# A new start-up order for a fused sliding-window attention and leaky-ReLU MLP: weights from the first microsecond, values last, sums ahead of values

## The chip, the cores and the metric

The kernel runs on one core of a Trainium2 chip. The metric is the device time of one execution in microseconds; lower is better. Five engines work side by side, each through its own list of instructions in the order in which the program gives them: TensorE (PE, matrix products, with its weight loads shown as PEld), VectorE (DVE), ScalarE (ACT), GpSimd (POOL) and SyncE (SP), which here only issues transfers. POOL and ACT issue some transfers too. All transfers run on the core's 16 DMA engines. Waits between engines are by semaphore.

## The reference

A sliding-window attention over 8 batches of 8 heads, 576 tokens and a head size of 64, and behind it an MLP on the 4608 tokens with 512 features, 2048 hidden units and a leaky ReLU:

```python
scores = scale * np.matmul(q, k.transpose(0, 1, 3, 2))
mask = np.abs(pos[:, None] - pos[None, :]) <= 32
scores = np.where(mask, scores, -1000000000.0)
attn = np.exp(scores - np.max(scores, axis=-1, keepdims=True))
attn = attn / (np.sum(attn, axis=-1, keepdims=True) + 1e-09)
x = np.matmul(attn, v)                  # (8, 8, 576, 64)
x = x.transpose(0, 2, 1, 3).reshape(4608, 512)
h = x @ w_in                            # 512 x 2048
out = np.maximum(0.01 * h, h) @ w_out   # 2048 x 512, float32
```

## The kernel before

**Tiling.** A unit of attention work has a number `i` from 0 to 63: batch `i // 8`, half of the sequence (288 tokens) `(i // 4) % 2`, and pair of heads `i % 4`; two heads (p and p+4) share the 128 partitions. Keys and values of a pair are laid out block-diagonally in `kbd` and `vbd` (two buffers each, for odd and even batches), nine blocks of 64 tokens. The zeros around the blocks are written once per buffer, by `clear` on ScalarE, a memset on VectorE (`kbd[0]`, L123), or memsets on POOL for the second buffers (L439, L454).

**One unit.** `cast_qk` (L167) turns loaded queries and keys into bfloat16, `transposes` (L186) turns them on TensorE, ScalarE copies the results out (L194 queries, L200 keys), and `place_keys` (L212, VectorE, two copies) puts the keys into `kbd`. `score(i)` makes five matmuls into `ps` (L227, one buffer), the exponential on ScalarE (L233, into `e`) and the product with the band mask on POOL (L237, into `pr`). `weighted(i)` makes the column sums by a matrix of ones (L261 and L264, or L259 where `join` has added the two parts beforehand, from unit 12 on), five value products into `x` (L271), the reciprocal of the sums on VectorE (L277) and the product `x * r` into `xT` (L279). `x` and `s` have one PSUM buffer each, and so each sum waits until the reciprocal before it has read `s`. `cast_v` copies values into `vbd`, on ScalarE (L175) in the start-up and on POOL (L177) later.

**The MLP.** For each half of a batch (288 tokens, group `g`) `h_tile(g, f)` makes four matmuls over the 512 features for each of 16 blocks `f` of hidden units (L290), and ScalarE's leaky ReLU writes `gT` (L294). `o_tile(j)` makes 16 matmuls of 512 columns for 128 tokens (L307), copies the sum out on ScalarE (L312) and stores it. The first `h_tile` of a half needs `xT` of all four pairs of that half.

**Order.** The schedule is written out by hand. The start-up runs from L88 to L424: loads on SP; constants; then casts, transposes and scores of batch 0 among each other; chunks of the weights (`load_w_in`, four chunks of 512 hidden units, two transfers each; `load_w_out`, four chunks) issued by POOL between its other work. These transfers convert from float32 to bfloat16. `keep_busy(n)` issues matmuls whose results nobody reads. Then come `h_tile(0, ·)` with units 4 to 7 between the tiles, and `h_tile(1, ·)` with the transposes of batch 1. Loads of batch 1 wait for weights by a transfer of four bytes that reads the weight tile (`behind` in `load_qk` and `load_v`).

After that a list `plan` holds the rest of the MLP's tiles with their costs, and `due` the times, in the plan's own clock of matmul time, at which `step()` does the next attention unit; `spend` compares the two before every four matmuls (0.864 of the plan's clock for output tiles). `step()` makes, in this order, the `join` of the next unit, transposes, `score(i + 2)`, `weighted(i)`, and the casts and loads that `PLAN` names.

Of the kernel before, what the change touches and what calls it, by code (L numbers as in the profile page):

```python
# [9 lines left out]
FP32 = mybir.dt.float32  # L10
# [6 lines left out]
def kernel(  # L17
# [12 lines left out]
    nc = tc.nc  # L30
# [18 lines left out]
    cast = ctx.enter_context(tc.tile_pool(name="cast", bufs=1))  # L49
    attn = ctx.enter_context(tc.tile_pool(name="attn", bufs=2))  # L50
    kt = ctx.enter_context(tc.tile_pool(name="kt", bufs=4))
    prob = ctx.enter_context(tc.tile_pool(name="prob", bufs=4))
    outp = ctx.enter_context(tc.tile_pool(name="outp", bufs=4))
    PS = bass.MemoryType.PSUM
    mmps = ctx.enter_context(tc.tile_pool(name="mmps", bufs=4, space=PS))
# [29 lines left out]
            )  # L85
        vf[b, p] = t

    load_qk(0, 0)  # L88
    load_qk(0, 1)
    load_v(0, 0)  # L90
    load_qk(0, 2)
    load_v(0, 1)
    load_qk(0, 3)
    load_v(0, 2)
    load_v(0, 3)


    ident_f = const.tile([128, 128], FP32)
# [18 lines left out]
    def clear(t, p):  # L117
        flat = t[:, p].rearrange("p n j -> p (n j)")
        nc.scalar.activation(
            out=flat, in_=zero.to_broadcast([128, NB * 128]), func=AF.Copy,  # L120
        )

    nc.vector.memset(kbd[0], 0.0)  # L123
    clear(vbd[0], 0)
    clear(vbd[0], 1)

# [3 lines left out]
    ]  # L132
    ODD = [32, 0]

    win = const.tile([128, 3, 128], BF16)
    nc.gpsimd.memset(win, 1.0)
    for lo in (0, 64):
        w = win[lo:lo + 64]
        nc.gpsimd.affine_select(
            out=w, in_=w, compare_op=ALU.is_ge, fill=0.0,  # L140
            base=0, channel_multiplier=-1, pattern=[[0, 3], [1, 128]],
        )
        nc.gpsimd.affine_select(
            out=w, in_=w, compare_op=ALU.is_ge, fill=0.0,
            base=2 * W, channel_multiplier=1, pattern=[[0, 3], [-1, 128]],
        )
    win_f = win.rearrange("p n c -> p (n c)")
    mask = [const.tile([128, NCOL], BF16, name=f"mask{i}") for i in range(2)]

    def make_masks():  # L150
        for hf in range(2):
            lo = W * (hf + 1)
            nc.gpsimd.tensor_copy(out=mask[hf][:, 0:HALF], in_=win_f[:, lo:lo + HALF])
            nc.gpsimd.tensor_copy(out=mask[hf][:, HALF:NCOL], in_=win_f[:, 0:NCOL - HALF])


    RING = 4 * HALF
    xT = const.tile([128, NPAIR, RING], BF16)
    w_in_bf = const.tile([128, DMC, DFF], BF16)
    w_out_bf = const.tile([128, FFC, DMODEL], BF16)  # L160


    qT = {}
# [55 lines left out]
    def where(i):  # L219
        return i // 8, (i // 4) % 2, i % 4  # L220

    def score(i):
        b, hf, p = where(i)
        ps = scps.tile([128, 1024], FP32, name="ps")
        c0 = 512 - HALF
        for blk, q0, n in WIN[hf]:
            nc.tensor.matmul(  # L227
                ps[:, c0:c0 + n], kbd[b % 2][:, p, blk],
                qT[b][:, p, q0:q0 + n], start=True, stop=True,
            )  # L230
            c0 += n
        e = attn.tile([128, NCOL], BF16, name="e")
        nc.scalar.activation(  # L233
            out=e, in_=ps[:, 512 - HALF:512 - HALF + NCOL], func=AF.Exp, scale=scale,
        )
        pr = prob.tile([128, NCOL], BF16, name="pr")
        nc.gpsimd.tensor_mul(pr, e, mask[hf])  # L237
        probs[i] = pr, None

    def join(i):  # L240


        hf = where(i)[1]
        pr = probs[i][0]
        both = prob.tile([128, HALF], BF16, name="both")
        o0 = ODD[hf]
        o1 = o0 + NCOL - HALF
        nc.vector.tensor_add(both[:, o0:o1], pr[:, o0:o1], pr[:, HALF:NCOL])  # L248
        rest = slice(0, o0) if o0 else slice(o1, HALF)
        nc.vector.tensor_copy(out=both[:, rest], in_=pr[:, rest])  # L250
        probs[i] = pr, both

    def weighted(i):
        b, hf, p = where(i)
        pr, both = probs.pop(i)
        x = xps.tile([128, HALF], FP32, name="x")
        s = xps.tile([128, HALF], FP32, name="s")
        if both is not None:
            nc.tensor.matmul(s, ones_bd, both, start=True, stop=True)  # L259
        else:  # L260
            nc.tensor.matmul(  # L261
                s, ones_bd, pr[:, 0:HALF], start=True, stop=False, skip_group_check=True,
            )
            nc.tensor.matmul(  # L264
                s[:, ODD[hf]:ODD[hf] + NCOL - HALF], ones_bd, pr[:, HALF:NCOL],
                start=False, stop=True, skip_group_check=True,
            )
        c0 = 0
        for n_, (blk, q0, n) in enumerate(WIN[hf]):
            a = q0 - HALF * hf  # L270
            nc.tensor.matmul(  # L271
                x[:, a:a + n], vbd[b % 2][:, p, blk, :], pr[:, c0:c0 + n],
                start=(n_ == 0), stop=(n_ == len(WIN[hf]) - 1), skip_group_check=True,
            )
            c0 += n
        r = attn.tile([128, HALF], FP32, name="r")
        nc.vector.reciprocal(r, s)  # L277
        t0 = (b * S + hf * HALF) % RING
        nc.vector.tensor_mul(xT[:, p, t0:t0 + HALF], x, r)  # L279

# [34 lines left out]
    def keep_busy(n):  # L315


        t = mmps.tile([128, 512], FP32, name="mm", tag="mm")
        for _ in range(n):
            nc.tensor.matmul(t, ones_bd, mask[0][:, 0:512], start=True, stop=True)  # L320


    NC = 2 * NPAIR * B
    JOINED = 12
    state = {"tp": 8, "done": 0}
    t_parts = {}


# [17 lines left out]
    def step():  # L346
# [7 lines left out]
        if b > 0:  # L354
            upto = 8 * (b + 1) + PLAN[b > 1][0][r]
            step_transposes(max(upto - 1, 8 * (b + 1)))
        if i < 7:
            score(i + 1)
        elif 8 <= i < NC - 2:
            score(i + 2)  # L360
        weighted(i)
        place_keys()
        if b > 0:
            step_transposes(upto)
# [9 lines left out]
        state["done"] += 1  # L374


    w_in_r = moe_w_in.rearrange("(a u d) f -> a d u f", a=2, d=D)
    w_out_r = moe_w_out.rearrange("(c p) f -> p c f", p=128)

    def load_w_in(f0, f1):  # L380
        for a in range(2):
            nc.gpsimd.dma_start(
                out=w_in_bf[64 * a:64 * a + 64, :, f0:f1], in_=w_in_r[a, :, :, f0:f1],
            )

    def load_w_out(i):
        c = slice(4 * i, 4 * i + 4)
        nc.gpsimd.dma_start(out=w_out_bf[:, c, :], in_=w_out_r[:, c, :])

    first = transposes(0)  # L390

    def first_pair():
        next(first)
        next(first)
        place_keys()

    cast_qk(0, 0, nc.vector)
    make_masks()
    cast_qk(0, 1, nc.vector)
    first_pair()  # L400
    first_pair()
    clear(vbd[0], 2)
    cast_v(0, 0)
    cast_qk(0, 2, nc.vector)
    score(0)
    load_w_in(0, 512)
    first_pair()
    clear(vbd[0], 3)
    cast_qk(0, 3, nc.vector)
    load_w_in(512, 1024)  # L410
    for i in range(NPAIR):
        score(i + 1)
        if i + 1 < NPAIR:
            cast_v(0, i + 1, on_act=True)
        if i < 2:
            load_w_in(1024 + 512 * i, 1536 + 512 * i)
        else:
            load_w_out(i - 2)
        if i > 0:
            keep_busy(3 if i == 1 else 2)  # L420
        weighted(i)
        if i == 0:
            first_pair()
    state["done"] = NPAIR  # L424

    for p in range(NPAIR):
        load_qk(1, p, w_in_bf[0:1, 0, 512:514] if p == 0 else None)
    keep_busy(2)  # L430
    step()
    load_w_out(2)
    load_w_out(3)
    for f in range(FFC):
        h_tile(0, f)
        if f in (2, 6, 10):
            step()
        if f % 4 == 3:
            nc.gpsimd.memset(kbd[1][:, f // 4], 0.0)  # L439
    cast_qk(1, 0, nc.vector)  # L440
    cast_qk(1, 1, nc.vector)
    for p in range(NPAIR):
        load_v(1, p, w_out_bf[0:1, 4, 0:2] if p == 0 else None)
    second = transposes(1)
    for f in range(FFC):
        h_tile(1, f)
        if f % 4 == 3:
            p = f // 4
            next(second)
            next(second)  # L450
            place_keys()
            if p + 2 < NPAIR:
                cast_qk(1, p + 2, nc.vector)
            nc.gpsimd.memset(vbd[1][:, p], 0.0)  # L454
        if f == 11:
            score(8)
    state["tp"] = 16
    score(9)
    for p in range(NPAIR):
        load_qk(2, p)  # L460

# [15 lines left out]
            at[g] = t  # L477
        t += us
    due = []
    for i in range(8, NC):  # L480
        prev = 0.9 * O_US * 4 if i < 12 else at[i // 4 - 1] - LEAD
        due.append(prev + (at[i // 4] - LEAD + (1.2 if i < 12 else 0) - prev) * (i % 4 + 1) / 4)
    clock = 0.0
    cast_v(1, 0)
    load_v(2, 0)

    def spend(us):
        nonlocal clock
        while due and due[0] <= clock:
            due.pop(0)  # L490
            i = state["done"]
            if i < 11:
                cast_v(1, i - 7)
                load_v(2, i - 7)
            step()
        clock += us

    for us, kind, g, f in plan:
# [33 lines left out]
```

## Time and profile before

| What | us |
|---|---|
| Median of 3 runs (lowest, highest) | 339.45 (339.32, 340.53) |
| The profiled execution, whole | 338.24 |
| its span, first to last instruction | 336.5 |
| TensorE busy (share) | 317.7 (94%) |
| VectorE, ScalarE, POOL busy | 232.6, 199.9, 180.3 |
| First matmul of any kind | 5.15 |
| First matmul of `h_tile(0, 0)` | 28.01 |
| First matmul of `o_tile(0)` | 48.73 |
| First matmul of `h_tile(2, 0)` | 69.58 |

The profiled execution was 1.21 us shorter than the median of the timed runs, 1.74 of it outside the span. A line of the profile's views names the engine and the kernel's line, `out<-in` by the names in the program, the shape and the count; in the views in order of time the first number is the start in microseconds from the start of the span and the second the length. What stands in square brackets is how long the engine had been idle, and what ended that. In the chain of waits every line is a piece of the chain that ended last, followed back from the end. A busy TensorE is not a TensorE at its peak, since the ends of matmuls are modelled and overlap; the distance between the starts of successive matmuls tells its pace.

### The profile page before, as it was taken

To read this page: it belongs to the slowest core of one execution; us is meant where nothing else is said; L and a number is where in the kernel's file an instruction comes from. 1 tells how busy PE (TensorE), PEld (TensorE's weight loads), DVE (VectorE), ACT (ScalarE), POOL (GpSimd) and SP (SyncE) were. 2 spreads that over 40 slices of the span, in tenths; PEclk is the share of its full clock that TensorE was granted. 3 is DMA by queue.
4 is the path that set the end of the run, shared out by engine and by line. 5 is a ranking of instruction groups with operands and counts; after the bars stand their busy time and mean duration, and the time that the engine had idled before them with its cause. 6 is when DMAs were issued, how large, how long until landed. Compare 5 with 4: busy or idle time off the path is not lost.

```text
span 336.5 us, 7011 instructions
## 1 busy us (share of the span) xinstructions
PE 317.7 (94%) x2725; PEld 215.6 (64%) x2725; DVE 232.6 (69%) x310; ACT 199.9 (59%) x432; POOL 180.3 (54%) x213
## 2 busy tenths in 40 slices
PE   2588999889999999999999999999999999999996
PEld 1346775466675767666675767667675766666653
DVE  5489653788768978797667978897677977666200
ACT  5775792275663856566564756567474656555441
POOL 7697658648755637565354646665363644221000
PEclk9999999999999999999999999999999999999999
DMA  8999989986794433553445423553311001010102
GB/s 186 215 201 222 270 195 213 268 199 178 183 180 148 139 94 99 157 163 73 126 127 156 135 68 107 165 178 73 106 29 64 33 2 62 2 62 3 62 2 94
DMA packets 60853, 42.40 MB, mean 126 GB/s; under 512 B 39700, under 2 KB 56340, under 8 KB 60820
## 3 DMA queue, kind: packets, MB, share of 16 engines
q1 hardware_dynamic: 51204, 28.32, 35.7%
q10 hardware_dynamic: 5328, 9.44, 7.8%
q0 software_dynamic: 4288, 4.20, 7.5%
q8 instruction: 21, 0.34, 0.4%
q14 instruction: 12, 0.10, 0.1%
HBM read 36.70 MB, written 9.44 MB: 137 GB/s over the span
## 4 chain that ended last, share of the span: by engine, by line
PE 83%; DMA 6%; DVE 5%; SPq 2%; ACT 2%; POOL 1%; issue 1%; ACTq 0%; DVEq 0%
PE mm L290 36%; PE mm L307 33%; PE tp L186 4%; PE x L271 4%; PE ps L227 4%; DVE r L277 3%; DMA kf<-in_k_dram 2%; DMA out_dram<-o_sb 2%; PE s L259 2%; DMA vf<-in_v_dram 2%; SPq L82 1%; SPq L71 1%; DVE xT L279 1%; ACT kT L200 0%; POOL vbd L177 0%
## 5 line engine op out<-in xcount | busy, mean ns | idle before, releaser
L277 DVE RECIPROCAL r<-s 128x288 f32<-128x288 f32 x64 | 125.2, 1957 | 55.4 <-PE s L259 47.3
L237 POOL TENSOR_TENSOR pr<-e,mask 128x544 bf16<-128x544 bf16 x64 | 77.6, 1214 | 111.9 <-ACT e L233 62.0
L290 PE MATMUL mm<-xT,w_in_bf 128*128 128x288 bf16 x1024 | 133.9, 286 | 0.0
L307 PE MATMUL mm<-w_out_bf,gT 128*128 128x512 bf16 (+2 forms) x592 | 130.1, 373 | 0.0
L290 PEld LDWEIGHTS <-w_in_bf 128*128 128x128 bf16 x1024 | 97.9, 98 | 24.8 <-issue 0.9
L294 ACT ACTIVATE gT<-mm 128x288 bf16<-128x288 f32 x256 | 99.9, 417 | 18.2 <-PE mm L290 6.7
L307 PEld LDWEIGHTS <-gT 128*128 128x128 bf16 x592 | 56.3, 98 | 59.8
L312 ACT ACTIVATE o_sb<-mm 128x512 f32<-128x512 f32 (+2 forms) x37 | 21.7, 586 | 81.3 <-PE mm L307 81.2
L233 ACT ACTIVATE e<-ps 128x544 bf16<-128x544 f32 x64 | 40.0, 625 | 27.1 <-PE ps L227 12.1
L177 POOL CAST vbd<-vf 64x576 bf16<-64x576 f32 x58 | 38.9, 670 | 2.5 <-DMA vf<-in_v_dram 0.6
L212 DVE COPY kbd<-kT 64x576 bf16<-64x576 bf16 x64 | 28.4, 444 | 11.2 <-ACT kT L200 10.6
L279 DVE TENSOR_TENSOR xT<-x,r 128x288 bf16<-128x288 f32 x64 | 29.3, 458 | 6.7
L167 POOL CAST kb<-kf 96x768 bf16<-96x768 f32 x32 | 27.5, 860 | 9.3 <-DMA kf<-in_k_dram 9.3
L248 DVE TENSOR_TENSOR both<-pr 128x256 bf16<-128x256 bf16 x52 | 27.0, 519 | 3.9 <-POOL pr L237 2.1
L227 PE MATMUL ps<-qT,kbd 128*128 128x128 bf16 (+2 forms) x320 | 26.8, 216 | 1.2 <-ACT e L233 1.2
L271 PE MATMUL x<-pr,vbd 128*128 128x128 bf16 (+2 forms) x320 | 26.3, 214 | 1.3 <-DVE xT L279 0.9
L227 PEld LDWEIGHTS <-kbd 128*128 128x128 bf16 x320 | 20.5, 101 | 8.8 <-issue 1.5
L271 PEld LDWEIGHTS <-vbd 128*128 128x128 bf16 x320 | 21.0, 100 | 5.9 <-issue 1.8
L250 DVE COPY both<-pr 128x32 bf16<-128x32 bf16 x52 | 24.6, 473 | 0.0
L194 ACT ACTIVATE qT<-tp 128x576 bf16<-128x576 bf16 x32 | 20.8, 651 | 3.3 <-PE tp L186 2.9
L200 ACT ACTIVATE kT<-tp 128x576 bf16<-128x576 bf16 x32 | 21.0, 656 | 2.9 <-PE tp L186 1.5
L186 PE MATMUL tp<-ident,qb 96*128 96x96 bf16 x192 | 14.4, 215 | 8.5 <-DVE qb L167 8.5
(37 smaller groups left out, 130.4 us busy)
## 6 DMA issues: line engine op xcount, KB each, us to landing
qf<-in_q_dram SPq DMA_DIRECT2D x32, 288.0 KB, 3.3
kf<-in_k_dram SPq DMA_DIRECT2D x32, 288.0 KB, 4.0
vf<-in_v_dram SPq DMA_DIRECT2D x64, 144.0 KB, 3.7
out_dram<-o_sb ACTq DMA_DIRECT2D x35, 256.0 KB, 2.5
w_in_bf<-in_moe_w_in_dram POOLq DMA_DIRECT2D x8, 256.0 KB, 6.5
w_out_bf<-in_moe_w_out_dram POOLq DMA_DIRECT2D x4, 512.0 KB, 11.9
out_dram<-o_sb ACTq DMA_DIRECT2D x1, 192.0 KB, 1.9
out_dram<-o_sb ACTq DMA_DIRECT2D x1, 64.0 KB, 1.6
```

What stands on the lines that cost most here:

```text
L177: nc.gpsimd.tensor_copy(out=vbd[b % 2][r, p, :, r], in_=vf[b, p][r])
L186: nc.tensor.transpose(tp[:, c], src[:, p, c].rearrange("p a d -> p (a d)"), ident[0:96, 0:96],)
L212: nc.vector.tensor_copy(out=kbd[b % 2][r, p, :, r], in_=kT[r].rearrange("p (n j) -> p n j", j=64),)
L227: nc.tensor.matmul(ps[:, c0:c0 + n], kbd[b % 2][:, p, blk], qT[b][:, p, q0:q0 + n], start=True, stop=True,)
L233: nc.scalar.activation(out=e, in_=ps[:, 512 - HALF:512 - HALF + NCOL], func=AF.Exp, scale=scale,)
L237: nc.gpsimd.tensor_mul(pr, e, mask[hf])
L271: nc.tensor.matmul(x[:, a:a + n], vbd[b % 2][:, p, blk, :], pr[:, c0:c0 + n], start=(n_ == 0), stop=(n_ == len(WIN[hf]) - 1), skip_group_c ...
L277: nc.vector.reciprocal(r, s)
L279: nc.vector.tensor_mul(xT[:, p, t0:t0 + HALF], x, r)
L290: nc.tensor.matmul(h[:, 0:HALF], w_in_bf[:, c, ts(f, 128)], xT[:, c, ds(t0, HALF)], start=(c == 0), stop=(c == DMC - 1),)
L294: nc.scalar.activation(out=gT[:, f, ds(t0, HALF)], in_=h[:, 0:HALF], func=AF.Prelu, alpha=0.01,)
L307: nc.tensor.matmul(o[:, lo:hi], gT[:, f, ds(128 * j % RING, 128)], w_out_bf[:, f, lo:hi], start=(f == 0), stop=(f == FFC - 1),)
```

## The change

Loads on SP: all queries and keys of batch 0 first, then all values. `load_w_in(0, 512)` is issued by POOL before everything else that POOL does; the other chunks and `w_out` follow between casts and mask products. `clear` runs for pairs 0 to 2 at the start. The band mask is made from one 128-column `win1` with four smaller selects, and VectorE copies it three times into `win`. For units 0 to 3 the mask product is taken in two parts straight from `win`, on VectorE for unit 3.

`weighted` is split into `sums` (sums and reciprocal) and `context` (value products and `x * r`). For units 0 to 3 `context` writes into the MLP's PSUM pool, and `r` gets four buffers, `pr` six. The start-up is written out unit by unit: sums are called before the values of the unit are cast. In the steady state `step` calls both one after the other.

```diff
+    for p in range(NPAIR):
+        load_qk(0, p)
+    for p in range(NPAIR):
+        load_v(0, p)
...
+    load_w_in(0, 512)
...
+    for p in range(NPAIR - 1):
+        clear(vbd[0], p)
     nc.vector.memset(kbd[0], 0.0)
-    clear(vbd[0], 0)
-    clear(vbd[0], 1)
...
+    nc.vector.tensor_copy(
+        out=win, in_=win1.rearrange("p (o c) -> p o c", o=1).to_broadcast([128, 3, 128]),
+    )
...
+        if i < NPAIR:
+            eng = nc.vector if i == 3 else nc.gpsimd
+            for lo, hi, at0 in PARTS[hf]:
+                eng.tensor_mul(pr[:, lo:hi], e[:, lo:hi], win_f[:, at0:at0 + hi - lo])
+        else:
+            nc.gpsimd.tensor_mul(pr, e, mask[hf])
...
+        r = recip.tile([128, HALF], FP32, name="r")
+        nc.vector.reciprocal(r, s)
+        probs[i][2] = r
+
+    def context(i):
+        b, hf, p = where(i)
+        pr, _, r = probs.pop(i)
+        if i < NPAIR:
+            x = mmps.tile([128, HALF], FP32, name="x0", tag="mm")
+        else:
+            x = xps.tile([128, HALF], FP32, name="x")
...
+        if i < NC - 2 and i not in (6, 7, 8, 9):
             score(i + 2)
-        weighted(i)
+        if probs[i][2] is None:
+            sums(i)
+        context(i)
```

The new start-up in full:

```python
cast_qk(0, 0, nc.vector)
load_w_in(512, 1024)
cast_qk(0, 1, nc.vector)
first_pair()
place_keys()
score(0)
cast_qk(0, 2, nc.vector)
first_pair()
place_keys()
score(1)
sums(0)
load_w_in(1024, 1536)
cast_qk(0, 3, nc.vector)
first_pair()
place_keys()
clear(vbd[0], 3)
score(2)
sums(1)
load_w_in(1536, 2048)
first_pair()
cast_v(0, 0, on_act=True)
place_keys()
make_masks()
score(3)
sums(2)
context(0)
cast_v(0, 1, on_act=True)
load_w_out(0)
keep_busy(4)
sums(3)
context(1)
score(4)
cast_v(0, 2, on_act=True)
load_w_out(1)
keep_busy(6)
context(2)
score(5)
cast_v(0, 3, on_act=True)
keep_busy(4)
context(3)
sums(4)
load_w_out(2)
load_w_out(3)
```

`keep_busy` now takes 288 columns a matmul, not 512, and writes `x`. Behind the start-up, queries, keys and values of batch 1 are loaded together, gated by the last chunk of `w_in`. In `h_tile(0, ·)` unit 4 to 7 come at f = 1, 5, 9 and 13: `context(i)`, then `sums(i + 1)` and `score(i + 2)`; POOL clears all of `kbd[1]` and `vbd[1]` there. `score(8)` and `score(9)` are made at f = 9 and 13 of `h_tile(1, ·)`.

Beside the first four output tiles, units 8 to 11 are divided in the `due` list: sums at 0.3, 2.4, 4.5 and 6.6 of the plan's clock (with `score(10)` and `score(11)`), then steps at 7.0, 8.7, 10.4 and 12.1, each with `cast_v(1, i - 8)` called just before it; `load_v(2, ·)` follows steps 11 to 14. Before, steps 8 to 12 fell into this stage; now unit 12 comes after it.

```diff
-    for i in range(8, NC):
-        prev = 0.9 * O_US * 4 if i < 12 else at[i // 4 - 1] - LEAD
-        due.append(prev + (at[i // 4] - LEAD + (1.2 if i < 12 else 0) - prev) * (i % 4 + 1) / 4)
+    for n in range(NPAIR):
+        due.append((0.3 + 2.1 * n, "sums"))
+    for n in range(NPAIR):
+        due.append((7.0 + 1.7 * n, "step"))
+    for i in range(12, NC):
+        prev = at[i // 4 - 1] - (LEAD if i >= 16 else 1.0)
+        due.append((prev + (at[i // 4] - LEAD - prev) * (i % 4 + 1) / 4, "step"))
```

## The prediction

> **What bounds the kernel now.** First I cut the span at the first matmul of the MLP's first product (28.01 us), at the first matmul of the output product (48.73) and at the start of half 2 (69.58), and read the view of busy time by stage. Its columns are the stretch, its length, and busy time with the number of instructions for PE, PEld, DVE, ACT and POOL, then the granted clock, the DMA share and GB/s.
>
> ```profile
> 0.00:28.01 28.01, 15.18 (x122) 9.61 (x123) 18.08 (x27) 18.07 (x25) 22.79 (x37) 1.00 1.12 201
> 28.01:48.73 20.72, 20.45 (x221) 16.74 (x218) 14.43 (x18) 16.89 (x42) 13.25 (x15) 1.00 1.05 234
> 48.73:69.58 20.85, 18.11 (x128) 9.41 (x125) 12.14 (x15) 7.07 (x12) 14.68 (x18) 1.00 1.12 240
> 69.58:300.00 230.42, 230.42 (x2028) 158.05 (x2025) 178.63 (x241) 141.37 (x315) 127.20 (x144) 1.00 0.40 110
> ```
>
> From 69.58 on TensorE never rests, and the change leaves that part alone. Between 28.01 and 48.73 it loses 0.27 us. So there are two places to win or lose: the start, and the 20.85 us of the first output tiles. Work in the latter, by the warm spacing of the rows: 64 output matmuls at 0.216 us (24 of them start 48.73 and the next operation starts by 53.9) is 13.8; five scores (L227) and five value products (L271) at 0.23, four sums at 0.24 and a joined one at 0.12 make 3.4; so 17.2, and 3.65 us are lost. The view of waits there finds few of them, since the modelled matmul ends cover the short ones:
>
> ```profile
> PE ps L227 <- ACT e L233: 1.2, 1, 1.2
> PE s L259 <- DVE r L277: 0.8, 1, 0.8
> PE x L271 <- DVE xT L279: 0.4, 2, 0.3
> ```
>
> Next the chain of waits (start, length, what), for what sets 28.01:
>
> ```profile
> 20.05 1.97 DVE r L277
> ...
> 22.74 1.97 DVE r L277
> ...
> 24.80 0.46 DVE xT L279
> 25.26 1.91 DVE r L277
> ...
> 27.26 0.46 DVE xT L279
> ```
>
> VectorE does a reciprocal and a product per pair, 2.45 us each, and the fourth product (27.26 to 27.72) lets the MLP start. No weight is waited for. The DMA engines are full as well (share 1.12), but the chain leaves DMA at 16.08, when the last keys land.
>
> Last, the timeline (start, length, engine, line, operation), for prices in the start-up, where matmuls run at half their later pace:
>
> ```profile
> 1.41 0.41 DVE L101 CAST ident<-ident_f 128x128 bf16<-128x128 f32 x1 [1.41 <-POOL ident_f masks.py:199]
> 2.70 1.98 DVE L123 MEMSET kbd<- 128x2304 uint32 x1 [0.43 <-issue]
> 4.60 0.49 DVE L167 CAST qb<-qf 96x768 bf16<-96x768 f32 x1
> 14.05 1.42 POOL L382 DMA_DIRECT2D w_in_bf<-in_moe_w_in_dram  x2
> 19.41 0.40 PE L261 MATMUL s<-pr,ones_bd 128*128 128x288 bf16 x1
> 20.27 0.66 PE L227 MATMUL ps<-qT,kbd 128*128 128x96 bf16 x5
> 21.02 0.62 ACT L233 ACTIVATE e<-ps 128x544 bf16<-128x544 f32 x1 [0.72 <-PE ps L227]
> 21.67 1.39 ACT L175 ACTIVATE vbd<-vf 64x576 bf16<-64x576 f32 x2
> ```
>
> From these and their neighbours: sums to value product 0.40, value product to next score 0.46, score start to exponential 0.75, sums start to reciprocal 0.64, reciprocal 1.96, exponential 0.62, pair of value casts 1.39, one transposed copy (L194, L200) 0.65, placing keys (two L212) 0.91, a value product to its end 0.66. Each engine runs its instructions in program order: ScalarE's clear at 10.09 goes ahead of an exponential whose scores were made at 9.23.
>
> **The change, part by part.**
>
> *Head.* Two weight DMAs now stand on POOL ahead of the identity: 1.42 us from the row at 14.05. The identity cast, which heads VectorE, and the memset of `kbd` follow: 4.12 to 6.10. The new copy of `win` (128x384) then precedes the first cast; nearest rows are 0.28 and 0.52 us (L248, 128x256), so 0.4. The first cast of queries starts at 6.5 instead of 4.60: **+1.9** (bounds 0, if POOL's issue were free, and +2.4). Cheaper selects on POOL and the clears on ScalarE (three at 1.1, 3.7 to 7.0) end before they are needed.
>
> *Arrival.* Rates by queue (packets, MB, share; q0 carries weights, q1 the rest), from the view of DMA cut to 32-44 us (weights beside keys) and to 16.5-20 (weights beside values):
>
> ```profile
> q0 software_dynamic: 1315, 1.31, 64.1%
> q1 hardware_dynamic: 1335, 1.90, 51.1%
> ```
>
> ```profile
> q0 software_dynamic: 471, 0.46, 80.9%
> q1 hardware_dynamic: 953, 0.23, 46.6%
> ```
>
> So keys get 158 and weights 109 KB/us together; values 66 and weights 131; alone, queries and keys 260 (2 to 6 us), values 190 (47 to 52). Weights flow 2.85 us after issue (14.05 to 16.9): chunk 0 from 3.6 to 8.4, chunk 1 (issued behind the first key cast) from 9.45 to 14.25. Queries and keys, 2.36 MB from 2.0, have 0.42 MB by 3.6, 1.18 by 8.4, 1.45 by 9.45, 2.21 by 14.25 and end at 14.85; with 1.35 us from last byte to use (1.33 for the old last keys), 16.2. Before it was 16.08: moving values behind them is eaten by the weights. Values then have 4.4 us alone (0.84 MB) until chunk 2 flows at 19.25, and 0.34 MB at 66: all landed by 25.9. That is ahead of their use, as the next paragraph shows, so both transfers cost nothing; values become late only if they land after 31.
>
> The Trainium skill's "DMA: Bandwidth & Descriptors", section "Queues, rings and completion order", has each DMA engine take turns between queues packet by packet. That holds at 32-44 us (1335 to 1315 packets), but beside values the row has 953 to 471. By equal turns values would get some 40 KB/us and land at about 29.3 (an estimate); the sum is the same by both.
>
> *Chain to the third reciprocal.* Place keys of pair 0 by 10.0 (3.5 after the cast, against 3.69 before). Then score 0, exponential to 11.4, queries and keys of pair 1 through ScalarE to 12.7, place to 13.6, score 1, sums 0, reciprocal 0 at 14.8. VectorE now has reciprocal 0, cast 3 (0.56) and placing 2 in a row: 1.96+0.56+0.91, score 2 0.46, sums 1 0.64 and the hand-overs: reciprocal 1 at 19.4. Then 1.96, placing 3 0.91, score 3 0.75, exponential 0.62, its mask product now on VectorE (two at 0.3): reciprocal 2 from 24.4 to **26.35**, against 24.70 before. Making sums early doesn't shorten it, because VectorE takes them in order among its casts and placings.
>
> *Tail.* Sums 3 have to wait for reciprocal 2 (one `s` buffer), and behind them on TensorE stand value product 1 and score 4; on ScalarE the order is exponential 4, cast of values 2, exponential 5, cast of values 3. Cold: sums 26.4, score 4 27.26, exponential 28.01 to 28.63, cast to 30.02, product 2 and score 5 30.54, exponential 31.29 to 31.91, cast to 33.30, product 3 34.01, `xT` to 34.50, MLP at 34.55. With warm rows (0.23 between groups, 0.51 from score to exponential) 33.17. Middle **33.9**, so **+5.9** on 28.01. The value casts, which used to lie under 2.45 us of VectorE per pair, are now in line with the exponentials, 3.3 us per pair.
>
> *First half of the MLP.* Value product 4 moves into it: +0.23. Reciprocal 4 starts only when `xT` 3 is done; sums 5 come two tiles and a product later (1.2 us) and wait for its 1.96: +0.75 (bounds 0 and 1.2). Next keys: gated by chunk 3 (issued at 21.0, landing 6.5 us later by the median, then up to the 4.5 us that the gate took, 23.13 to 27.65), flowing from about 34, pairs landing 5 us later and every 3.7: 39 to 50; they are wanted from 46.9 every 2.4. `w_out` by 50 and values of batch 1 by 56.5 are wanted at 55 and 66. Hidden with 3 us to spare. The memsets moved on POOL lie in its idle time.
>
> *Output tiles.* Sums fall due at 0.3, 2.4, 4.5, 6.6 of matmul time, steps at 7.0 to 12.1, taken at multiples of 0.864. The last placing of keys ends 2.1 after the stage starts, so reciprocal 8 ends at 4.06 and sums 9 wait 0.8; sums 11 wait 0.45. Value casts 0 to 2 run early, but the fourth is issued behind mask product 12, which ends at 16.7; cast 1.38, and product 11 waits 1.35. So 13.8+2.8 of work and 2.6 lost, 19.25, with step 12 (0.6) now after it: against 20.85, **-1.0** (bounds -3.65, all waits gone, and +1).
>
> Sum: 5.9+0.23+0.75-1.0 = **+5.9 us**. The profiled execution took 338.24 (span 336.5), so 344.1; the median of the runs is 339.45, 1.21 more, and with the same +5.9 **345.3**.
>
> **The rivals.** What a measurement can tell from no change is 0.5%, 1.7 us (337.75 to 341.15).
>
> *Values are last, and everything else is ready* (faster). Then the start ends with landing 25.9, cast 1.39, product 0.66, `xT` 0.46 and hand-overs, 28.45: +0.4, and with 0.23, 0.75 and all of the 3.65 won, -2.2: 337.2. For it: DMA share 1.12. It decides only if reciprocal 2 ends by 21.6, since 6.8 us follow it even warm; one of the two loops of 4.6 and 5.0 would have to drop out. Chance 0.09.
>
> *TensorE cold at the MLP's start.* Before, it ran nearly dense from 17.92 (dummy matmuls of 512 columns 0.43 apart), and the groups are warm from 22.63 on. Now idle gaps of 1.7, 0.9 and 1.4 us lie in the last 8 us, with 14 dummy matmuls of 288 columns among them. If 4.7 us run at half pace, +2.35; from the cold start (34.55, +0.65) and without the 0.75 of sums 5 that makes +8.2: 347.6. Chance 0.20. The Trainium skill's "TensorE: Matmul & The Clock Gate", part 1 on the clock gate, speaks against this change too: full clock comes after a busy window of some 3.4 us and goes after an idle one. The granted clock here reads 1.00 throughout, so the pace of the rows must decide; by the page the loss would be 1.7 and the time about 347.0, an estimate.
>
> *Head nearly free and output tiles clean.* If POOL's issue and the copy cost 0.4 rather than 1.9, and the output tiles win 3.0: +2.4, so 341.8; with the sums 5 hidden as well 341.1. Chance 0.12, a third of it within 0.5%.
>
> *The early weights bring nothing by themselves*: part of every case, as the MLP never waited for them.
>
> **How the numbers follow.** The forecast has 0.59, and its own range is 342.5 to 347. With both lower rivals and the cold one, 8 in 10 lie between 340.8 and 348.8. Faster 0.08 (nearly all of the first rival), same 0.08 (the rest of it, a third of the third, and misses of the forecast), slower 0.84.
>
> **What would show it.** Right: the first query cast near 6.5; reciprocal 2 ending near 26; two exponential-then-cast pairs on ScalarE in the last 6 us before the MLP; MLP near 34; a wait for product 11 on the value cast. Wrong: MLP before 30, values landing after 31, reciprocal 2 before 22, or MLP matmuls 0.24 apart for several us.

## The result, and the profile after

The changed kernel takes 351.93 us (median of 4 runs, 350.91 to 353.38), the kernel before 339.38 beside it: 1.0365 of the time before, with a 95% interval from 1.0319 to 1.0410. It is slower by 12.55 us, where 5.9 were forecast, and outside the range.

The view of busy time by stage of the changed kernel, cut at the same events as before (its columns as in the prediction), with one cut more between the two halves of batch 0 and one at half 3:

```profile
0.00:37.47 37.47, 15.39 (x123) 11.41 (x124) 18.16 (x29) 19.43 (x27) 21.08 (x39) 1.00 0.98 183
37.47:49.84 12.37, 12.37 (x102) 9.64 (x100) 10.04 (x10) 7.17 (x17) 8.31 (x9) 1.00 1.15 248
49.84:61.73 11.89, 10.77 (x125) 8.77 (x123) 8.11 (x10) 10.38 (x27) 8.00 (x9) 1.00 1.15 218
61.73:81.45 19.72, 17.16 (x115) 8.87 (x113) 11.35 (x12) 5.62 (x10) 10.87 (x13) 1.00 0.43 114
81.45:101.65 20.20, 19.05 (x177) 13.28 (x176) 15.95 (x23) 12.80 (x28) 13.71 (x17) 1.00 0.78 180
101.65:351.70 250.05, 245.88 (x2099) 167.03 (x2097) 174.62 (x232) 146.20 (x328) 116.00 (x131) 1.00 0.34 96
```

The second number of each line, set against the same stretch before (from the starts of the first matmul of each stage in the two traces):

| stage | before | after | difference |
|---|---|---|---|
| to the MLP's first matmul | 28.01 | 37.47 | +9.46 |
| first product, half 0 | 10.35 | 12.37 | +2.02 |
| first product, half 1 | 10.37 | 11.89 | +1.52 |
| first four output tiles | 20.84 | 19.72 | -1.12 |
| half 2 with its output tiles | 18.27 | 20.20 | +1.93 |
| the rest | 248.68 | 250.05 | +1.37 |
| span | 336.5 | 351.7 | +15.2 |

0.6 us of the last stages but one are only moved (unit 12, from the output tiles into half 2), so these are -0.5 and +1.3. The profiled execution of the changed kernel was the longest of its four, 1.45 us over the median, and that of the kernel before 1.14 under its median; hence 15.2 in the spans and 12.55 in the medians. Five of six stages lose, and three of them are stages that the forecast had at nothing.

The start-up in the timeline (start, length, what; in brackets the idle time before it and what ended that):

```profile
1.33 1.42 POOL L102 DMA_DIRECT2D w_in_bf<-in_moe_w_in_dram  x2 [0.81 <-POOLq L567]
...
6.65 0.54 DVE L187 CAST qb<-qf 96x768 bf16<-96x768 f32 x1
...
10.89 0.56 DVE L187 CAST qb<-qf 96x768 bf16<-96x768 f32 x1 [3.70 <-DMA qf<-in_q_dram]
...
13.14 0.82 POOL L187 CAST kb<-kf 96x768 bf16<-96x768 f32 x1 [5.81 <-DMA kf<-in_k_dram]
...
27.59 1.95 DVE L295 RECIPROCAL r<-s 128x288 f32<-128x288 f32 x1
```

The first cast is where it was worked out (6.65, forecast 6.5). The next, of pair 1, waits 3.70 us for its queries, which by the rates of the prediction were to be there at 7.8, and the keys come at 13.1 instead of 9.7. Reciprocal 2 (the one of unit 2) ends at 29.54 instead of 26.35. From there on ScalarE, in the same view for that engine alone:

```profile
31.23 0.62 ACT L253 ACTIVATE e<-ps 128x544 bf16<-128x544 f32 x1 [2.69 <-PE ps L247]
31.88 1.39 ACT L195 ACTIVATE vbd<-vf 64x576 bf16<-64x576 f32 x2
34.49 0.62 ACT L253 ACTIVATE e<-ps 128x544 bf16<-128x544 f32 x1 [1.23 <-issue]
35.14 1.39 ACT L195 ACTIVATE vbd<-vf 64x576 bf16<-64x576 f32 x2
```

Two times exponential, then cast, 3.26 us apart, just ahead of the MLP: the tail as forecast (7.93 us from the reciprocal to the MLP, worked out 8.2 cold and 6.8 warm).

### The profile page after: what moved, and what is told of

Same layout as the page of the kernel before. It is cut to its first block, busy times and chain, and to the rows that moved or that the text cites. A ratio compares the mean times of both kernels' runs of the same rounds, so it can differ in the third digit from the quotient of the medians.

```text
span 351.7 us, 7037 instructions
## 1 busy us (share of the span) xinstructions
PE 320.6 (91%) x2730; PEld 219.0 (62%) x2730; DVE 238.2 (68%) x313; ACT 201.6 (57%) x434; POOL 178.0 (51%) x213
## 3 DMA queue, kind: packets, MB, share of 16 engines
q1 hardware_dynamic: 51202, 28.32, 34.0%
## 4 chain that ended last, share of the span: by engine, by line
PE 76%; POOL 5%; ACT 5%; DVE 2%; issue 2%; ACTq 0%; POOLq 0%; DVEq 0%
PE mm L342 32%; PE mm L325 31%; PE x L308 4%; PE ps L247 4%; PE tp L206 3%; PE s L285 2%; POOL vbd L197 2%; ACT e L253 1%; ACT gT L329 1%; POOL vbd L479 1%; DVE r L295 1%; POOL pr L263 1%; ACT kT L220 1%; ACT vbd L195 1%; POOL kbd L479 1%
## 5 line engine op out<-in xcount | busy, mean ns | idle before, releaser
L263 POOL TENSOR_TENSOR pr<-e,mask 128x544 bf16<-128x544 bf16 x60 | 73.0, 1216 | 125.9 <-ACT e L253 79.0
L325 PE MATMUL mm<-xT,w_in_bf 128*128 128x288 bf16 x1024 | 136.2, 288 | 0.0
L325 PEld LDWEIGHTS <-w_in_bf 128*128 128x128 bf16 x1024 | 98.8, 99 | 25.9 <-issue 0.9
L197 POOL CAST vbd<-vf 64x576 bf16<-64x576 f32 x56 | 37.6, 671 | 4.7 <-DMA vf<-in_v_dram 2.1
L247 PE MATMUL ps<-qT,kbd 128*128 128x128 bf16 (+2 forms) x320 | 27.5, 220 | 12.1 <-DVE kbd L232 10.0
L247 PEld LDWEIGHTS <-kbd 128*128 128x128 bf16 x320 | 20.8, 102 | 20.2 <-DVE kbd L232 13.2
L274 DVE TENSOR_TENSOR both<-pr 128x256 bf16<-128x256 bf16 x52 | 29.1, 559 | 6.3 <-POOL pr L263 4.4
L232 DVE COPY kbd<-kT 64x576 bf16<-64x576 bf16 x64 | 28.3, 443 | 5.6 <-ACT kT L220 5.1
```

The lines of the kernel that those rows point to most:

```text
L197: nc.gpsimd.tensor_copy(out=vbd[b % 2][r, p, :, r], in_=vf[b, p][r])
L232: nc.vector.tensor_copy(out=kbd[b % 2][r, p, :, r], in_=kT[r].rearrange("p (n j) -> p n j", j=64),)
L247: nc.tensor.matmul(ps[:, c0:c0 + n], kbd[b % 2][:, p, blk], qT[b][:, p, q0:q0 + n], start=True, stop=True,)
L325: nc.tensor.matmul(h[:, 0:HALF], w_in_bf[:, c, ts(f, 128)], xT[:, c, ds(t0, HALF)], start=(c == 0), stop=(c == DMC - 1),)
```

## The experiments

Ratios are to the kernel before, run on the same chip, with their 95% intervals; the changed kernel itself has 1.0365 (1.0319 to 1.0410). Where a run tells of a stage, that is from its trace, with this table's columns: end of reciprocal 2, start of the MLP, then the lengths of the two halves of the first product, of the output tiles, of half 2 and of the rest.

| run | recip. 2 | MLP | half 0 | half 1 | output | half 2 | rest |
|---|---|---|---|---|---|---|---|
| before | 24.7 | 28.01 | 10.35 | 10.37 | 20.84 | 18.27 | 248.68 |
| changed | 29.5 | 37.47 | 12.37 | 11.89 | 19.73 | 20.20 | 250.03 |
| weights as late as before | 25.1 | 33.01 | 12.13 | 11.89 | 19.72 | 20.20 | 250.09 |
| casts first | 29.4 | 34.96 | 11.55 | 11.90 | 19.73 | 20.20 | 250.07 |
| values of batch 2 early | 29.7 | 36.75 | 11.64 | 11.90 | 19.73 | 20.20 | 248.75 |
| memsets back | 28.2 | 35.33 | 11.16 | 10.42 | 19.72 | 20.21 | 250.12 |
| weights behind the mask | 24.6 | 32.52 | 12.23 | 11.89 | 19.72 | 20.20 | 249.99 |
| small transfers ahead | 26.4 | 34.28 | 12.14 | 11.89 | 19.73 | 20.21 | 249.22 |
| old spacing | 28.3 | 35.60 | 11.99 | 11.90 | 20.32 | 18.27 | 249.58 |
| all five | 24.7 | 29.80 | 11.17 | 10.42 | 20.33 | 18.27 | 248.74 |
| sums ahead alone | 23.6 | 26.88 | 10.35 | 10.42 | 25.42 | 18.50 | 248.68 |
| sums ahead, tuned | 24.0 | 27.45 | 11.26 | 10.42 | 19.57 | 18.27 | 249.09 |
| and values of batch 1 early | 24.6 | 27.95 | 10.35 | 10.76 | 18.88 | 18.27 | 249.19 |
| and stores by SP | 24.2 | 27.56 | 10.35 | 10.77 | 18.05 | 18.27 | 249.17 |
| stores by SP alone | 25.0 | 28.32 | 10.35 | 10.37 | 17.88 | 18.27 | 248.68 |

The start differs between executions of the same code: in the five profiles that leave it as changed up to there (changed, casts first, values of batch 2 early, memsets back, old spacing), reciprocal 2 ends between 28.2 and 29.7 us. So the stages of a run tell more than its MLP start alone.

**Weights as late as before.**

```diff
-    load_w_in(0, 512)          # ahead of all else on POOL
...
     score(0)
+    load_w_in(0, 512)
...
     sums(0)
-    load_w_in(1024, 1536)
+    load_w_in(512, 1024)
```

> The changed kernel with its weight transfers issued as late as before the change: chunk 0 behind score 0, chunks 1 to 3 each one place later. Nothing of the computation changes. Theory A (early weights delay queries and keys, and the start is a chain behind them): the query cast of pair 1 starts near 7 instead of 10.9 us, reciprocal 2 ends near 25 instead of 29.5, the MLP starts near 33 instead of 37.5; time 347 to 348.5 instead of 351.9. Rival (all the bytes have to come before the MLP anyway, DMA engines full): the MLP starts within 1 us of 37.5 and the time stays at 351 to 353.

Ratio 1.0279 (1.0253 to 1.0306), 348.36 us. The MLP starts 4.5 us sooner, as the first theory had it (33.01). All the bytes have to come before the MLP, but not beside the first queries.

**Value casts ahead of the exponentials.**

```diff
     context(1)
+    cast_v(0, 2, on_act=True)
+    cast_v(0, 3, on_act=True)
     score(4)
-    cast_v(0, 2, on_act=True)
...
     score(5)
-    cast_v(0, 3, on_act=True)
```

> The changed kernel with the value casts of pairs 2 and 3 ahead of scores 4 and 5 on ScalarE. Theory A (exponentials 4 and 5 stand before those casts, and nothing else holds value products 2 and 3): the 7.9 us from the end of reciprocal 2 to the MLP shrink to about 4, time 347.5 to 349. Rival (values land too late for casts to run earlier, or TensorE's own cold work fills the tail): the tail shrinks by less than 1.5 us, time 350.5 or more.

Ratio 1.0323 (1.0297 to 1.0349). The tail falls from 7.93 to 5.6 us: 2.4 of the 3.9 that were expected. ScalarE in the timeline of that run:

```profile
27.00 4.21 ACT L195 ACTIVATE vbd<-vf 64x576 bf16<-64x576 f32 x6
31.23 0.62 ACT L253 ACTIVATE e<-ps 128x544 bf16<-128x544 f32 x1
33.38 0.62 ACT L253 ACTIVATE e<-ps 128x544 bf16<-128x544 f32 x1 [1.53 <-issue]
```

The casts now run in one block that ends at 31.2, before the value products need them. What is left is TensorE at its slow pace: ten dummy matmuls, 0.24 us apart, stand in line between reciprocal 2 and the MLP. What the tail takes without them wasn't tried.

**Values of batch 2 early.**

```diff
                     cast_v(1, i - 8)
+                    load_v(2, i - 8)
                 step()
-                if 11 <= i < 15:
-                    load_v(2, i - 11)
```

> The changed kernel with the values of batch 2 loaded at units 8 to 11, as before the change, and not behind units 11 to 14. Theory A (a late value load holds POOL at 103 us, and behind it a mask product, a join and a cast): the stretch from the second half of batch 1 on loses its 2 us of TensorE idle time, time 349 to 350.5. Rival (those waits come from VectorE's reciprocals, which the new spacing of units 12 on has moved): no change, 351 to 353.

Ratio 1.0375 (1.0350 to 1.0399): by the time nothing can be told. By the trace the rest falls from 250.05 to 248.75, what it was before (248.68), and two waits of the changed kernel are gone. These are a wait of POOL in its timeline and one of TensorE in the view of waits (total, times, longest):

```profile
105.36 0.66 POOL L197 CAST vbd<-vf 64x576 bf16<-64x576 f32 x1 [2.08 <-DMA vf<-in_v_dram]
```

```profile
PE ps L247 <- DVE kbd L232: 1.1, 2, 1.0
PE tp L206 <- POOL qb L187: 0.7, 1, 0.7
```

The last line is absent in this run; the one above stays (1.2), so the 20.20 us of half 2 have another cause. How much the late loads cost differs from run to run: where they stay late and the spacing stays new, the rest takes from 249.22 us (small transfers ahead) to 250.12, so 0.5 to 1.4 more than here.

**Memsets back.**

```diff
-        if f % 2 == 1:
-            nc.gpsimd.memset((kbd if f < 8 else vbd)[1][:, f // 2 % 4], 0.0)
+        if f % 4 == 3:
+            nc.gpsimd.memset(kbd[1][:, f // 4], 0.0)
...
             second_pair(f // 4)
+            nc.gpsimd.memset(vbd[1][:, f // 4], 0.0)
```

> The changed kernel with POOL's memsets of the second buffers where they stood before the change: key buffer at f = 3, 7, 11, 15 of the first half, value buffer behind the transposes of batch 1. Theory A (eight memsets in a row delay the key casts of batch 1, and slow VectorE's casts beside them): the first transposes of batch 1 no longer wait (1.3 us), time 350 to 351. Rival (queries and keys of batch 1 land late themselves): no change, 351 to 353.

Ratio 1.0338 (1.0304 to 1.0371). Half 1 falls from 11.89 to 10.42. In the changed kernel POOL, VectorE and TensorE stood like this in their timelines:

```profile
48.31 4.05 POOL L479 MEMSET vbd<- 128x1152 bf16 x4
52.32 3.77 POOL L187 CAST kb<-kf 96x768 bf16<-96x768 f32 x4
```

```profile
49.44 4.43 DVE L187 CAST qb<-qf 96x768 bf16<-96x768 f32 x2
```

```profile
52.84 0.43 PE L206 MATMUL tp<-ident,qb 96*128 96x96 bf16 x6 [0.87 <-DVE qb L187]
53.51 0.43 PE L206 MATMUL tp<-ident,kb 96*128 96x96 bf16 x6 [0.24 <-POOL kb L187]
```

The key casts queue behind four memsets, and the query casts on VectorE take 4.43 us for two, against 1.49 before; the first alone takes 3.34 us and ends at 52.78, 0.4 us after the memsets (52.36). TensorE waits first for that query cast (0.87 us) and then for the key cast (0.24). The run removes both waits at once and does not tell them apart.

Half 0 has a share of it too: with one slow matmul each, it takes 11.64 us in the run before this one and 11.16 here. The mask product of unit 7 stands behind two memsets there and one here, and POOL starts it 6.98 us into the half there and 6.49 here.

**Weights behind the mask, and small transfers in their place.** The two are one test. The first issues two transfers 1.55 us later (at 2.88, not 1.33), and their first bytes come 4.1 us later (at 7.9, not 3.7). The second puts two small transfers where they were.

```diff
-    load_w_in(0, 512)
+    scrap = const.tile([64, 2, 2], BF16)      # second run alone
+    for a in range(2):
+        nc.gpsimd.dma_start(out=scrap[:, a], in_=w_in_r[a, :, 0, 0:2])
...
+    load_w_in(0, 512)
     win_f = win.rearrange("p n c -> p (n c)")
```

> The changed kernel with the first two weight transfers issued by POOL behind the identity and the band mask, some 3.5 us later, and nothing else moved. Theory A (head and arrival add up, as the prediction had it): the first query cast at 4.7 instead of 6.7 us and reciprocal 2 ends about 2 us sooner, 27.5; time some 2 us under the changed kernel, 1.030 to 1.033 of the kernel before. Rival (arrival alone decides, since the first placing of keys stands behind the query cast of pair 1, which waits for its bytes until 10.9): the first cast is at 4.7, but the query cast of pair 1 gains only what the weights start later, less than 1.5 us, and reciprocal 2 ends at 28.3 or later.

> As the run with the weights behind the mask, but with two transfers of 64 x 2 numbers into a scrap tile where the first weights had been issued: the head's delay on POOL without the bytes. Theory A (the bytes beside queries and keys delay pairs 0 and 1; the head alone gives what the prediction worked out): first query cast 6.3 to 6.7, query cast of pair 1 before 8.5, reciprocal 2 ends at 26 to 27, 1.5 to 2 us later than with no transfer ahead; ratio 1.027 to 1.031. Rival (the issue ahead of the identity does the harm by itself): query cast of pair 1 after 10, reciprocal 2 ends at 28.5 or later, ratio 1.035 or more.

Ratios 1.0240 (1.0223 to 1.0258) and 1.0283 (1.0260 to 1.0306). Without the weights ahead reciprocal 2 ends at 24.6, with small transfers ahead at 26.35, with the weights themselves at 29.54. Both theories of the first run were too low: it won 4.9 us, not 2 and not 1. The head is worth 1.8 (1.9 in the prediction), the bytes 3.2, and between 1.9 and 3.3 by the five profiles with the weights ahead. VectorE with small transfers:

```profile
6.48 1.24 DVE L190 CAST qb<-qf 96x768 bf16<-96x768 f32 x2
...
24.40 1.95 DVE L298 RECIPROCAL r<-s 128x288 f32<-128x288 f32 x1
```

Here pair 1 is cast right behind pair 0, and the chain to reciprocal 2 ends at 26.35, the very figure of the prediction, though its steps were off by some tenths each. And the DMA view from 4 to 8 us, for the changed kernel and then for small transfers ahead (packets, MB, share):

```profile
q0 software_dynamic: 288, 0.28, 57.0%
q1 hardware_dynamic: 332, 0.47, 43.7%
```

```profile
q1 hardware_dynamic: 767, 1.08, 106.0%
q0 software_dynamic: 158, 0.00, 5.1%
```

Beside weights queries and keys get 0.47 MB in those 4 us, not 1.08, and both queues together only 0.75: 188 KB/us, where the same pair of queues moved 268 at 32 to 44 us before. By the shares and counts of these lines a packet of weights took 0.127 us there, and 0.094 at 32 to 44 us.

The trace holds sixteen landing marks for each load, and a load is complete with the last of them. For the keys of pair 1 the first comes at 8.31 in the changed kernel, the twelfth at 10.35 and the last at 13.09; with small transfers ahead all sixteen lie between 6.84 and 7.38. All five profiles with the weights ahead have such a spread for these keys, from 3.7 to 4.9 us.

**Old spacing.**

```diff
-        prev = at[i // 4 - 1] - (LEAD if i >= 16 else 1.0)
+        prev = at[i // 4 - 1] - LEAD
```

> The changed kernel with units 12 to 15 due from four microseconds of the plan's clock before half 2, as before the change, instead of one. Theory A (the denser spacing asks VectorE for a unit of some 4.9 us every 4.1): the 20.2 us from half 2 to half 3 fall to about 18.3, those of the output tiles grow by 0.6 for unit 12, and the time falls by 1.3 us, to 1.032 to 1.034 of the kernel before. Rival (the dense stretch is moved, not widened: VectorE is as late in any spacing): both stages together, 39.9 us, stay within 0.4.

Ratio 1.0318 (1.0297 to 1.0339). Output tiles 20.32 and half 2 18.27, together 38.6 against 39.9: 1.3 us, as the first theory said. Units 12 to 15 ask VectorE for reciprocal, product, join and placing more often than it can give them: in the changed kernel two reciprocals in a row stand 4.92 us apart (92.98 and 97.90), with VectorE busy for 4.3 of them, and the wait "PE ps L247 <- DVE kbd L232" shown above is absent with the old spacing.

**All five.** The runs above in one kernel, with the weights behind the mask.

> The changed kernel with five things undone or turned round at once: first weights behind the mask, value casts 2 and 3 ahead of scores 4 and 5, memsets and values of batch 2 where they stood, units 12 to 15 at the old spacing. If the five costs add: reciprocal 2 ends at 24.7, MLP at 30.3, first half 11.3, second 10.4, output tiles 20.3, half 2 18.3, rest 248.7: span 339.2 against 336.5, ratio 1.006 to 1.010. Rival (they overlap, and one undone lets another wait appear): ratio over 1.013.

Ratio 1.0052 (1.0034 to 1.0070), just under the range that adding gave; span 338.7 against 339.2 worked out, and every stage within 0.5 us of it. The costs add.

**The sums ahead of values, alone.** The kernel before, with `weighted` split in two and the `due` list of the changed kernel for units 8 to 11; then with due times that keep a reciprocal between sums and with the four value casts in a row; then with the values of batch 1 loaded earlier; then also with the first four stores issued by SP.

```diff
-    for i in range(8, NC):
-        prev = 0.9 * O_US * 4 if i < 12 else at[i // 4 - 1] - LEAD
+    due = [
+        (0.3, "sums"), (3.4, "sums"), (6.0, "sums"), (7.7, "step"),
+        (8.6, "sums"), (10.3, "step"), (11.2, "step"), (12.9, "step"),
+    ]
...
-            nc.scalar.dma_start(out=out[ts(j, 128), lo:hi], in_=o_sb[:, lo:hi])
+            (nc.sync if j < 4 else nc.scalar).dma_start(out=out[ts(j, 128), lo:hi], in_=o_sb[:, lo:hi])
```

> The kernel before with one part of the change alone: sums and reciprocals of units 8 to 11 ahead of their value products, due at the changed kernel's times, scores 8 and 9 at f = 9 and 13. Start-up, memsets, loads and units from 12 on as before. Theory A (the part brings what its working out says): the output tiles' stage, 20.8 us before, takes 20.3 (19.7 as in the changed kernel and 0.6 for unit 12, which stays inside): ratio 0.996 to 1.001. Rival (that part is a loss of its own): the stage takes 21 or more, ratio over 1.002.

> The same part alone, with its waits taken out by other due times: sums at 0.3, 3.4, 6.0 and 8.6, steps at 7.7, 10.3, 11.2 and 12.9 (each sum a reciprocal and its hand-over apart), and all four value casts of batch 1 on POOL ahead of mask product 12. Theory A (the 3.65 us lost in the output tiles are waits between VectorE, POOL and TensorE): the stage takes 17.5 to 18.5 us, ratio 0.991 to 0.994. Rival (the loss is contention or late values and doesn't go with the order): the stage takes 20 or more, ratio 0.998 or above.

> The kernel before with the tuned sums-ahead part and with the values of batch 1 loaded right behind its queries and keys, without the gate on the output weights. Theory A (late value casts are what is left of the wait): value product 8 no longer waits 1.9 us, the output tiles' stage takes 17.5 to 18.5 us instead of 19.6. Rival (ScalarE is held, when it issues the store of an output tile, by loads that SP has under way, and exponentials 11 and 12 come late behind it): the exponential after the first store still starts some 3 us late and the stage takes 19 or more.

> The same with the stores of the first four output tiles issued by SP, not by ScalarE. Theory A of the run before (nothing holds ScalarE): no difference to it, within 0.5 us in that stage. Rival (the issue of the store holds ScalarE): exponentials 10 to 13 follow their scores within 0.6 us and the stage takes 16.9 to 17.9; ratio to the kernel before 0.990 to 0.993.

Ratios 1.0084 (1.0055 to 1.0112), 1.0019 (0.9996 to 1.0042), 0.9961 (0.9938 to 0.9984) and 0.9904 (0.9885 to 0.9923). The first does not take 20.3 us for the output tiles but 25.4, and the tuned one 19.6, not 18: both miss. With the values of batch 1 early it is 18.88, between theory and rival, and with the stores by SP 18.05, near the rival's 16.9 to 17.9. Why the first two miss, ScalarE's timeline of the first shows:

```profile
61.70 0.60 ACT L323 ACTIVATE o_sb<-mm 128x512 f32<-128x512 f32 x1 [4.04 <-PE mm L318]
66.06 0.37 ACTq L324 DMA_DIRECT2D out_dram<-o_sb  x1
66.53 0.62 ACT L235 ACTIVATE e<-ps 128x544 bf16<-128x544 f32 x1 [4.23 <-DMA kf<-in_k_dram]
```

The output tile is copied by 62.30, but its store is issued at 66.06, and the exponential behind it, whose scores were made at 62.4, waits 4.23 us. The kernel before has the same:

```profile
52.39 0.60 ACT L312 ACTIVATE o_sb<-mm 128x512 f32<-128x512 f32 x1 [2.09 <-PE mm L307]
55.81 0.37 ACTq L313 DMA_DIRECT2D out_dram<-o_sb  x1
56.28 0.62 ACT L233 ACTIVATE e<-ps 128x544 bf16<-128x544 f32 x1 [3.30 <-POOL vbd L177]
```

2.8 us between copy and store, and an exponential behind. What held it stands in the chain of waits before:

```profile
50.34 5.40 DMA vf<-in_v_dram
...
55.75 0.02 ACTq L313
...
55.81 6.94 DMA out_dram<-o_sb
```

The queue of ScalarE waits there (ACTq) until a load of values, issued by SP at 50.34, has landed at 55.73, and issues the store right after it. The data of the store has nothing to do with that load. In the trace both have the same landing semaphore: the transfers of SP and ScalarE take eight of them in turn, and each waits until the transfer that had its semaphore last has landed. In the first run above it is a load of keys, issued at 56.16 and landed at 65.99. In the changed kernel the store follows its copy by 0.03 us (67.43 and 0.60, then 68.06), since the load with its semaphore had landed at 60.34: the loads of the next batches are through by then, as the stage starts 13 us later (DMA share 0.43 against 1.12).

**Stores by SP, alone.** The last line of the diff above and nothing else, on the kernel before.

> The kernel before with one line changed: SP issues the stores of the first four output tiles. Theory A (what the kernel before lost in that stage is ScalarE held at the issue of a store by the loads of batches 1 and 2 under way): exponentials follow their scores within 0.7 us, and the stage of 20.8 us takes 18.5 to 19.5 in spite of its old order; ratio 0.993 to 0.997. Rival (the order of sums and value products is the larger part, the store the smaller): the stage takes 20 or more, ratio 0.998 or above.

Ratio 0.9882 (0.9862 to 0.9901), 335.36 us against 339.19: faster than expected, and the lowest ratio of all, though its interval overlaps that of the run before it. So the sums ahead of values, even tuned, add nothing to it that these runs can tell. The output tiles take 17.88 us, with 17.2 of work. ScalarE:

```profile
52.69 0.60 ACT L312 ACTIVATE o_sb<-mm 128x512 f32<-128x512 f32 x1 [2.09 <-PE mm L307]
54.72 0.62 ACT L233 ACTIVATE e<-ps 128x544 bf16<-128x544 f32 x1 [1.43 <-PE ps L227]
```

The exponential now waits for its scores only. SP issues the first of these stores at 59.78, 6.5 us after the copy, once the load with its semaphore has landed (59.72). The wait now stands in SP's list, and no exponential is behind it.

## Why the prediction was wrong, point by point

| term | forecast | measured |
|---|---|---|
| head, to reciprocal 2 | +1.9 | +1.8 |
| arrival beside the weights | 0 | +3.2 (1.9 to 3.3 by run) |
| tail, reciprocal 2 to MLP | 7.55 us | 7.93 us |
| half 0: product 4 and sums 5 | +0.98 | +0.8 |
| half 0: memsets on POOL | 0 | +0.5 |
| half 0: slow pace of TensorE | 0 (a rival: +2.35) | +0.7 in this run |
| half 1, memsets on POOL | 0 | +1.5 |
| output tiles | -1.0 | -0.5 |
| half 2 and the rest | 0 | +1.3 and +1.4 |

The sign, the place of the largest loss and its mechanism were right: the start is a chain through VectorE's order, its head is held by POOL's issue, and the value casts stand in line behind exponentials. The measured 0.8 of half 0 is 11.16 less 10.35, from the run with the memsets back, which has one slow matmul there; 11.64 with the memsets moved and one slow matmul gives the next 0.5, and 12.37 the 0.7 of the slow pace.

The step that failed worst is "all landed by 25.9 ... so both transfers cost nothing". It took rates from 32 to 44 us and a lag of 1.35 us from last byte to use, and set both into the first ten microseconds. There, queries and keys get 118 KB/us beside weights and not 158, and they lag: the hardware queue had moved 1.23 MB by 9.3 us, more than the 1.18 of pairs 0 and 1, but the keys of pair 1 are cast only at 13.14, with POOL idle. Half of their landing marks are there by 9.21, so the mean rate was not far off; the last of the sixteen, at 13.09, is what the cast waits for. The forecast had followed the last byte of all, and the chain hangs on pair 1. Small transfers in the weights' place give the forecast's 26.35, so the bytes, not the issue, make the 3.2. Why the two queues together move only 188 KB/us there, and why some parts of a load come so much later than others, wasn't tried and stays open. The values, worked out to be landed by 25.9, landed at 28.5, still ahead of the 31 that the prediction named.

The second is "From 69.58 on TensorE never rests, and the change leaves that part alone". Two edits of the diff reach into it: the spacing of units 12 to 15 (1.3, by the old spacing) and the value loads of batch 2, issued behind a step and so behind the next queries and keys (1.3 by the trace of the early load, 0.5 to 1.4 over the runs). The prediction described both and priced neither.

The third is "The memsets moved on POOL lie in its idle time". They did, but the casts and the mask product next in POOL's line did not, and VectorE's query cast was stretched beside them (1.5 in half 1 and 0.5 in half 0, by the memsets put back).

The output tiles came out near their term, but partly by luck, on a wrong reading of the kernel before. The waits worked out for the changed kernel did come (0.9, 0.3 and, for the last value cast, 1.3 us in the view of waits of that stage, 2.5 in all, forecast 2.6). But the 3.65 us of the kernel before were put down to short waits for VectorE, and the profile's own line for the longest, 3.30 us of ScalarE "<-POOL vbd", names an engine that had nothing to do with it. The held store was in the timeline, 2.8 us between copy and issue, and in the chain of waits; the run with the stores moved shows that it was 3 of the 3.65. The changed kernel's gain there may be no more than that its stage starts after the loads have drained. Set against the old order with the stores moved (17.88 us), the changed order with unit 12 inside (20.33) looks like a loss of some 2.4; it wasn't tried alone with the store free.

Of the rivals, the cold TensorE was half right. In the runs that leave the code of half 0 as changed, it took between 11.55 and 12.37 us, and between 1 and 12 of 48 matmul distances were of the slow kind (over 0.18 us). The granted clock of half 0 read 1.00 in all of them but one, also in the run with 12; in the run with the old spacing it read 0.87, with 6. The tail differs the same way, from 7.1 us, where the last three of eight distances between dummy matmuls are 0.12 us, to 7.9, where all are 0.24. The Trainium skill's "TensorE: Matmul & The Clock Gate", part 1, says that the window that decides runs free of the kernel, so that the count of slow matmuls changes from run to run; these rows agree with it. The faster rival needed reciprocal 2 by 21.6, and no run that keeps the new start-up came under 24.6. The third needed a head of 0.4, and it is 1.8.

## What to carry to other kernels

In a start-up, a transfer that is needed later should not be issued beside the first transfers of the chain: here bytes in the queue ahead cost more than the average rate said, and what counted was when the last part of an early pair landed, not the last byte of all. Before a reordered stage is priced, follow each engine's list of instructions past the end of the stage, and price each change of a due time or of a load's place in its queue. Where a wait's named releaser has nothing to do with the waiting instruction, look at the instruction just before it on that engine: a store that can't be issued holds everything behind it, and what holds it can be the landing of a load that has nothing to do with it.

## What the runs showed of the hardware that was not expected

A store from ScalarE was held for 2.8 to 3.8 us by the landing of a load from SP with the same landing semaphore (55.81 after a copy that ended at 52.99; 66.06 after 62.30), and for 0.03 us when that load had landed before; issued by SP, the first four stores made the kernel 1.2% faster. This is a wait of the program, not of the DMA engines.

A query cast on VectorE (96x768), 0.56 us by itself, took 3.34 us beside POOL's memsets of the value buffer and ended 0.4 us after them; beside POOL's key casts, in the run with the memsets back, it took up to 1.48. The Trainium skill's "GPSIMD Engine Reference", section 1, has the two engines share their SBUF interfaces, with contention for some VectorE instructions. The rows agree with it, as far as two of them can.

In the first microseconds two queues together moved 0.75 MB in 4 us, where one alone moved 1.08, and the sixteen parts of one load, the keys of pair 1, landed 3.7 to 4.9 us apart, where they lay 0.5 us apart with small transfers in the weights' place. The Trainium skill's "DMA: Bandwidth & Descriptors", section "Queues, rings and completion order", has each DMA engine take turns between queues packet by packet; the near equal packets (288 and 332) agree.
